# Attention and MLP on one core: who copies the sink probabilities, and how many steps the attention runs ahead

## The chip, the core and the metric

The program runs on one core of a Trainium2 chip. Times are device microseconds (us) of one execution; a kernel's time is the median of its runs. The engines are called as in the profile: PE (TensorE matmul), PEld (its weight load), DVE (VectorE), ACT (ScalarE), POOL (GpSimd) and SP (SyncE, which issues most DMAs).

## What is computed

A masked attention with 4 batches, 8 heads, 768 positions and head size 64, whose output is laid out as 3072 rows of 512 and put through an MLP:

```python
keep = is_sink | in_window            # 4 sink positions, window 128
scores = np.where(keep, q @ k.T / sqrt(64), -1e9)
a = softmax(scores)
x = (a @ v)  ->  (3072, 512)
h = x @ w_in                          # 512 x 2048
out = np.maximum(0.01 * h, h) @ w_out # 2048 x 512
```

## The kernel before

The rows are cut into eight **units** `u` of 384 rows (half of a batch, three tiles of 128 queries). A unit needs its attention for 8 heads, in 4 pairs, and then its MLP. The kernel writes both as Python generators, and every `yield` ends a **step**. PE executes its instructions in the order in which they are written (`tc.manual_schedule(engines=MANUAL)`); the order on DVE, ACT, POOL and SP is made at build time by a scheduler, which places instructions by its own forecast. At run time each engine takes its instructions strictly in that order.

*The MLP of a unit* (`mlp_stream`) goes through 16 blocks `fc` of 128 hidden columns. One block is seven steps: four of three matmuls into the PSUM tile `h` (L601), then three of three matmuls into `o` (L627) that use the block before. Between them ACT makes `g = 0.01 h` (L608), DVE `g = max(h, g)` (L609), ACT the rounded `gh` (L610), and DVE (POOL in unit 0) the rest `gl` (L611). `h` has one PSUM bank: the first matmul of the next `h` waits for L609 of this one. The names below give unit and block: `g3_2` is unit 3, block 2.

*The attention* (`attention_stream`) has 15 steps for a pair of heads: six `scores` (L293, then on DVE L311 and L319, on ACT `exp` L322, on DVE L323, L324, L328), six `tail` (a transpose L367 into `t`, L374 on ACT, L375 on DVE, L337 on POOL), one `sinks` (L388, L395, L408 to L410) and two `values` (L448 and L458 into `v`, then L462 on ACT and L463 on DVE to `xf`, and for the second head L465 on POOL, L467 on DVE, `xh` L557 on ACT and `xl` L558 on DVE). Units 0 and 1 have another, cheaper form of attention (L285, L305, L307, L490, L356, L359, L421, L425). Q, K and V of the later units are split into two parts by ACT and POOL (L243, L244, L246; L257, L258; L260, L261), with one buffer for `vsp` (L257) and `ssp` (L260).

*How the two are woven together* is a formula: after MLP step `x` the attention stream is advanced until it has made `due` steps.

```python
if x < mlp_steps:
    due = early_steps + LEAD0 + (early_steps + LEAD - LEAD0) * (x + 1) // mlp_steps
else:
    due = 2 * early_steps + LEAD + att_steps * (x + 1 - mlp_steps) // mlp_steps
```

Here `early_steps` is 32, `att_steps` 60, `mlp_steps` 112 and `LEAD0` 7. So 37 attention steps go into the MLP of unit 0, and 60 into each MLP of units 1 to 6, one after every 28/15 MLP steps. As 28 steps are four blocks and 15 steps are one pair, the picture repeats every four blocks: a pair's `values` stand at the same place of blocks 1 and 2, 5 and 6, 9 and 10, 13 and 14.

The copy that is changed stands in `tail`: after the last tile of a head it gathers the probabilities of the four sink columns from `pk` into `sk`, 128 x 8 or 128 x 12 elements, 48 times. `sk` is read by the transpose L388. In units 2 to 5, `check_weights` reads every weight again and tests its range (L194 on ACT, L196 on POOL, L198 on DVE, through two shared buffers), one weight block after each odd `fc`.

Of the kernel before, what the change touches and what calls it, by code (L numbers as in the profile page):

```python
# [27 lines left out]
T = 3  # L28
# [3 lines left out]
NSK = 4  # L32
# [8 lines left out]
MASKED = 1.0e38  # L41
DEEP = 9.0e8
SO = 3
LEAD = 12
LEAD0 = 7
SAHEAD = 2
NACT = 4
# [71 lines left out]
def fast_path(ctx, tc, cpool, qp, qk, vu, vs, w_in, w_out, out, ident, lims, negm, wmin, wmax):  # L119
    nc = tc.nc  # L120
# [214 lines left out]
    def place(out, src, x, prev):  # L335
        sign = -1 if prev else 1
        nc.gpsimd.affine_select(out=out, in_=src, pattern=([[0, x]] if x > 1 else []) + [[sign, P]],  # L337
                                base=-1 if prev else 0, channel_multiplier=-sign, compare_op=ALU.is_ge, fill=0.0)
# [4 lines left out]
    def slot():  # L343
        slots[0] += 1
        n = slots[0]
        if phase[0] == 0 and n % 2:
            return ps_h.tile([P, 512], F32, tag="h", name=f"t{n}")
        return ps_t.tile([P, 512], F32, tag="d" if phase[0] == 2 and n % 2 else "t", name=f"t{n}")
# [15 lines left out]
    def tail(u, h, j, pk, pt, sk):  # L364
        half = u % 2
        tp = slot()
        nc.tensor.transpose(out=tp[:, 0:P], in_=pk[:, j, NSK:], identity=ident)  # L367
        if j or half:
            o = 2 * P * j if half else (2 * j - 1) * P
            stg = apool.tile([P, 2, P], F32R, tag="stg", name=f"stg{u}_{h}_{j}")  # L370
            hi, lo = stg[:, 0, :], stg[:, 1, :]
        else:
            o, hi, lo = None, pt[:, 0, 0:P], pt[:, 1, 0:P]
        nc.scalar.copy(out=hi, in_=tp[:, 0:P])  # L374
        nc.vector.tensor_tensor(out=lo, in0=tp[:, 0:P], in1=hi.bitcast(F32), op=ALU.subtract)  # L375
        if o is not None:
            for prev in (1, 0):
                place(pt[:, :, o + (1 - prev) * P:o + (2 - prev) * P], stg, 2, prev)
        if j == T - 1:
            nj = T - 1 + half  # L380
            nc.vector.tensor_copy(out=sk[:, 0:nj, h % 2], in_=pk[:, T - nj:, 0:NSK])

    def sinks(u, pair, sk, state):
        half = u % 2
# [139 lines left out]
    def attend_late(u, h, pend, state):  # L524
        odd = h % 2
        sp = split_head(u, h)
        state = state[h // 2 % 2]
        if odd:
            state["v"] = split_values(u, h - 1)
        else:  # L530
            state["sk"] = apool.tile([P, T, 2, NSK], F32, tag="sk", name=f"sk{u}_{h // 2}")
        load_next(u, h)
        pk = apool.tile([P, T, WM], F32, tag="pk", name=f"pk{u}_{h}", bufs=PKB)
        sk = state["sk"]
        pt = apool.tile([P, 2, 2 * TU], F32R, tag="pt", name=f"pt{u}_{h}")
        state["pt", odd] = pt
        for j in range(T):
            ps = scores(u, h, j, (0, TU + NK[u % 2]), sp)
            softmax(u, h, j, ps, pk[:, j, :])
            yield  # L540
            at = len(pend) - (VSW and j == 0 and not odd and len(pend) > 0)
            pend.insert(at, (0, lambda j=j: tail(u, h, j, pk, pt, sk)))
# [123 lines left out]
    for x, _ in enumerate(mlp_stream()):  # L666
        if x >= mlp_steps:
            phase[0] = 2
# [4 lines that stand above are left out]
        while done < due:  # L673
# [204 lines left out]
```

## Time and profile before

| | |
|---|---|
| median of 3 runs | 699.86 us (699.4 to 700.22) |
| the profiled execution, its own time | 699.75 us |
| its span, first to last instruction | 698.0 us |
| PE busy / DVE / ACT / POOL | 98% / 77% / 62% / 57% of the span |
| granted clock of TensorE | 0.998 of full speed |
| MLP of unit 0 begins | 36.6 us |
| MLPs of units 1 to 7 begin (first L601 of each) | 125.8, 206.9, 291.3, 373.4, 458.1, 540.1, 621.8 us |

The share outside the span is 1.75 us. Matmuls are pipelined: a matmul of `h` is shown 0.34 us long, but the next one starts 0.175 us after it. So about 0.165 us of a wait of PE hide under the modelled end of the matmul before it.

### The profile page before, as it was taken

The numbers are of one execution on the slowest core, as the hardware profiler recorded it, in microseconds if no ns is written. First come the engines' busy times: TensorE is split into PE (matmuls) and PEld (weight loads), VectorE is DVE, ScalarE is ACT, GpSimd is POOL, SyncE is SP. The second block draws the span as 40 slices with busy tenths as digits, with TensorE's granted clock in tenths as the row PEclk, the third lists the DMA queues.
The fourth block names the chain that finished last, engine by engine and source line by source line (L and its number), as shares of the span: only waits on it lengthen the run. The fifth ranks groups of instructions, "written<-read, shape, count | busy, mean of one in ns | idle before, by whom it ended". The sixth has DMA issues, their size and how long they took to land.

```text
span 698.0 us, 12481 instructions
## 1 busy us (share of the span) xinstructions
PE 684.3 (98%) x3869; PEld 598.0 (86%) x3869; DVE 537.0 (77%) x1732; ACT 430.7 (62%) x1182; POOL 400.6 (57%) x550
## 2 busy tenths in 40 slices
PE   8999999999999999999999999999999999999996
PEld 5467788889998899988998899998999999899995
DVE  6999898666788898978898888887888988642322
ACT  6987676576666666667666667666676665522221
POOL 3357678465567877576775877757767665400000
PEclk9999999999999999999999999999999999999999
DMA  7865672212215423344333433333432310000001
GB/s 223 286 199 183 220 231 87 92 39 66 72 50 181 139 79 116 96 140 122 118 108 123 151 84 117 111 111 123 125 103 77 119 53 17 1 31 16 0 1 49
DMA packets 42599, 74.28 MB, mean 106 GB/s; under 512 B 3488, under 2 KB 26272, under 8 KB 42528
## 3 DMA queue, kind: packets, MB, share of 16 engines
q1 hardware_dynamic: 42384, 73.31, 33.3%
q8 instruction: 32, 0.52, 0.3%
q14 instruction: 39, 0.32, 0.2%
q10 hardware_dynamic: 144, 0.13, 0.1%
HBM read 67.14 MB, written 6.29 MB: 105 GB/s over the span
## 4 chain that ended last, share of the span: by engine, by line
PE 86%; DVE 5%; ACT 3%; POOL 2%; DMA 2%; issue 1%; POOLq 0%; ACTq 0%; SPq 0%; DVEq 0%
PE h L601 36%; PE o L627 34%; PE v L458 4%; PE s L293 4%; PE t L367 2%; PE v L421 1%; PE s L285 1%; ACT pe L307 1%; PE o_s L627 1%; PE o_o L627 1%; DMA ciraw<-in_w_in 1%; DVE pe L305 1%; ACT qksp L243 1%; DMA coraw<-in_w_out 1%; DVE g L609 0%
## 5 line engine op out<-in xcount | busy, mean ns | idle before, releaser
L601 PE MATMUL h<-xh,wi 128*128 128x384 f32 x1024 | 311.1, 352 | 1.9 <-DVE sm L323 1.2
L627 PE MATMUL o<-wo,gh 128*128 128x512 f32 x736 | 234.8, 400 | 0.2 <-ACT gh L610 0.2
L601 PEld LDWEIGHTS h<-xh,wi 128*128 128x128 f32 x1024 | 189.9, 188 | 17.4 <-issue 3.1
L601 PE MATMUL h<-xl,wi 128*128 128x384 f32 x512 | 172.8, 338 | 0.2 <-DVE xl L558 0.2
L337 POOL TENSOR_SCALAR_AFFINE_SELECT pt<-stg 128x256 fp32r<-128x256 f32 x240 | 101.1, 446 | 83.9 <-DVE stg L375 57.8
L627 PE MATMUL o<-wo,gl 128*128 128x512 f32 x368 | 145.4, 395 | 0.4 <-POOL gl L611 0.4
L627 PEld LDWEIGHTS o<-wo,gh 128*128 128x128 f32 x736 | 126.4, 188 | 16.7 <-issue 1.3
L609 DVE TENSOR_TENSOR g<-h,g 128x384 f32<-128x384 f32 x128 | 71.0, 555 | 54.9 <-ACT g L608 53.1
L608 ACT ACTIVATE g<-h 128x384 f32<-128x384 f32 x128 | 62.3, 487 | 66.5 <-PE h L601 65.8
L601 PEld LDWEIGHTS h<-xl,wi 128*128 128x128 f32 x512 | 96.9, 189 | 3.0 <-DVE xl L558 0.6
L610 ACT CAST gh<-g 128x384 fp32r<-128x384 f32 x128 | 65.2, 510 | 32.1 <-DVE g L609 30.6
L627 PEld LDWEIGHTS o<-wo,gl 128*128 128x128 f32 x368 | 69.1, 188 | 18.0 <-POOL gl L611 1.1
L322 ACT ACTIVATE pk<-pk,negm 128x128 f32<-128x128 f32 (+1 forms) x144 | 58.3, 405 | 36.8 <-DVE negm L319 35.9
L611 DVE TENSOR_TENSOR gl<-g,gh 128x384 fp32r<-128x384 f32 x112 | 69.8, 623 | 11.6 <-ACT gh L610 9.9
L244 POOL TENSOR_TENSOR qksp<-qkraw,qksp 64x392 fp32r<-64x392 f32 (+1 forms) x48 | 59.0, 1228 | 29.3 <-ACT qksp L243 16.2
L374 ACT CAST stg<-t 128x128 fp32r<-128x128 f32 x120 | 31.2, 260 | 53.0 <-PE t L367 50.5
L293 PEld LDWEIGHTS s<-qksp 128*128 128x128 f32 x288 | 53.3, 188 | 7.0 <-issue 0.6
L293 PE MATMUL s<-qksp 128*128 128x260 f32 (+1 forms) x288 | 56.2, 277 | 0.3 <-DVE negm L319 0.3
L328 DVE TENSOR_SCALAR pk<-pk,sm 128x132 f32<-128x132 f32 (+1 forms) x120 | 52.2, 435 | 3.1
L246 POOL TENSOR_TENSOR qksp<-qkraw,qksp 128x384 fp32r<-128x384 f32 x48 | 51.3, 1068 | 3.8
L311 DVE COPY_PREDICATED s<-tri,s 128x128 f32<-128x128 int8 x120 | 34.7, 289 | 16.6 <-PE s L293 15.4
L319 DVE CUSTOM_DVE_ANT_0 pk<-s,m 128x128 f32<-128x128 f32 (+1 forms) x144 | 41.7, 290 | 4.6 <-PE s L293 2.2
(149 smaller groups left out, 1119.7 us busy)
## 6 DMA issues: line engine op xcount, KB each, us to landing
qkraw<-in_qk SPq DMA_DIRECT2D x24, 454.0 KB, 3.3
qkraw<-in_qk SPq DMA_DIRECT2D x24, 388.0 KB, 3.1
wiraw<-in_w_in SPq DMA_DIRECT2D x16, 512.0 KB, 4.1
woraw<-in_w_out SPq DMA_DIRECT2D x16, 512.0 KB, 3.7
ciraw<-in_w_in SPq DMA_DIRECT2D x16, 512.0 KB, 3.7
coraw<-in_w_out SPq DMA_DIRECT2D x16, 512.0 KB, 3.5
out<-ob SPq DMA_DIRECT2D x23, 256.0 KB, 2.0
vraw<-in_vu SPq DMA_DIRECT2D x14, 256.0 KB, 2.6
```

The lines of the kernel that those rows point to most:

```text
L244: nc.gpsimd.tensor_tensor(out=sp[D:P, TU:TU + n], in0=raw[D:P, TU:TU + n], in1=sp[D:P, TU:TU + n].bitcast(F32), op=ALU.subtract)
L246: nc.gpsimd.tensor_tensor(out=sp[:, TU + n:2 * TU + n], in0=raw[:, 0:TU], in1=sp[:, 0:TU].bitcast(F32), op=ALU.subtract)
L293: nc.tensor.matmul(ps[:, 0:kn], lhsT=sp[:, off + j * P:off + (j + 1) * P], rhs=sp[:, TU + k0:TU + k0 + kn], start=c == 0, stop=c == len(pa ...
L322: nc.scalar.activation(out=w, in_=w, func=AF.Exp, scale=-1.0, bias=neg, accum_out=sm)
L328: nc.vector.tensor_scalar(out=w, in0=w, scalar1=sm, scalar2=None, op0=ALU.mult)
L337: nc.gpsimd.affine_select(out=out, in_=src, pattern=([[0, x]] if x > 1 else []) + [[sign, P]], base=-1 if prev else 0, channel_multiplier= ...
L601: nc.tensor.matmul(ph[:, 0:TU], lhsT=w[:, cs], rhs=x, start=cc == 0 and c == 0, stop=cc == NCC - 1 and c == 2)
L608: nc.scalar.mul(g, ph[:, 0:TU], 0.01)
L609: anchor[0] = nc.vector.tensor_tensor(out=g, in0=ph[:, 0:TU], in1=g, op=ALU.max)
L610: nc.scalar.copy(out=gh, in_=g)
L611: (nc.gpsimd if u == 0 else nc.vector).tensor_tensor(out=gl, in0=g, in1=gh.bitcast(F32), op=ALU.subtract)
L627: nc.tensor.matmul(acc, lhsT=gg[:, tsl], rhs=w[:, cs], start=f == 0 and c == 0, stop=f == NFC - 1 and c == 2)
```

## The change

Two lines. `LEAD` goes from 12 to 13: from unit 1 on the attention has made one step more at each MLP step, and unit 0 takes 38 attention steps, not 37. And the copy into `sk` is issued on ScalarE (ACT), not on VectorE (DVE). It stands in `tail`, which only units 2 to 7 use.

```diff
-LEAD = 12
+LEAD = 13
@@ tail
         if j == T - 1:
             nj = T - 1 + half
-            nc.vector.tensor_copy(out=sk[:, 0:nj, h % 2], in_=pk[:, T - nj:, 0:NSK])
+            nc.scalar.copy(out=sk[:, 0:nj, h % 2], in_=pk[:, T - nj:, 0:NSK])
```

What this does to the orders is seen best at the second `values` of a pair. On PE, in the MLP of unit 3 (block 2, with the attention of unit 4), before the change; `v4_1` is the second head's values, `s4_3_1` a score of the next pair, `h3_2` the block's hidden tile:

```order
L293 MATMUL s4_3_0_4201<-qksp4_3_4183 128x128 x2
L601 MATMUL h3_2_4169<-xh3_3_3935,wi2_633 128x384
L601 MATMUL h3_2_4169<-xl3_3_3936,wi2_633 128x384
L601 MATMUL h3_2_4169<-xh3_3_3935,wi2_633 128x384
L448 MATMUL t109_4220<-st0_100,ssp4_0_3889 128x256
L458 MATMUL v4_1_4222<-pt4_1_3901,vsp4_0_3888 128x256 x5
L627 MATMUL o3_0_4141<-wo1_548,gh3_1_4125 128x512 x2
```

The same place on PE with the change:

```order
L448 MATMUL t109_4210<-st0_100,ssp4_0_3883 128x256
L458 MATMUL v4_1_4212<-pt4_1_3895,vsp4_0_3882 128x256 x5
L601 MATMUL h3_2_4173<-xh3_3_3925,wi2_633 128x384
L601 MATMUL h3_2_4173<-xl3_3_3926,wi2_633 128x384
L601 MATMUL h3_2_4173<-xh3_3_3925,wi2_633 128x384
L293 MATMUL s4_3_1_4236<-qksp4_3_4177 128x260 x2
L627 MATMUL o3_0_4150<-wo1_548,gh3_1_4135 128x512 x2
```

The values have moved from behind the last matmuls of `h3_2` to before them, and the next score, formerly between the `o` matmuls, now follows `h3_2` directly.

On DVE, the instructions ahead of `g3_2` (L609, which frees the bank of `h3_2`), before the change:

```order
L198 ISA zeroi4_4165,wmin_64<-magi4_4164,zeroi4_4165 128x512
L198 ISA wmin_64 128x1
L375 TENSOR_TENSOR pt4_2_4020<-t108_4173,pt4_2_4020 128x128
L319 ISA pk4_3_4199,negm_63<-s4_3_0_4201,m0_115 128x128
L319 ISA negm_63 128x1
L609 TENSOR_TENSOR g3_2_4213<-h3_2_4169,g3_2_4213 128x384
```

With the change:

```order
L328 TENSOR_SCALAR pk4_3_4193<-pk4_3_4193,sm4_3_0_4198 128x128
L311 COPY_PREDICATED s4_3_1_4236<-tri_116,s4_3_1_4236 128x128
L319 ISA pk4_3_4193,negm_63<-s4_3_1_4236,m1_620 128x132
L319 ISA negm_63 128x1
L463 TENSOR_TENSOR xf4_0_4147<-v4_1_4212,xf4_0_4147 64x512
L609 TENSOR_TENSOR g3_2_4229<-h3_2_4173,g3_2_4229 128x384
```

The mask and maximum of the new score (L311, L319) and the sum of the values (L463) now stand ahead of L609; before, they stood behind it.

On ACT at the opening of unit 0's MLP (`gh0_0` is what the first `o` waits for), before the change:

```order
L608 ACTIVATE g0_0_659<-h0_0_646 128x384
L182 CAST wi2_633<-wif2_629 128x512
L359 COPY pt1_0_482<-t23_666 128x2x256
L490 ACTIVATE pe1_1_0_587<-pe1_1_0_587,sm1_1_585 128x260 x2
L610 CAST gh0_0_660<-g0_0_659 128x384
L490 ACTIVATE pe1_1_1_607<-pe1_1_1_607,sm1_1_585 128x260 x2
L608 ACTIVATE g0_1_709<-h0_1_693 128x384
```

With the change:

```order
L359 COPY pt1_0_482<-t23_656 128x2x256
L608 ACTIVATE g0_0_666<-h0_0_646 128x384
L182 CAST wi2_633<-wif2_629 128x512
L490 ACTIVATE pe1_1_0_587<-pe1_1_0_587,sm1_1_585 128x260 x2
L490 ACTIVATE pe1_1_1_607<-pe1_1_1_607,sm1_1_585 128x260 x2
L608 ACTIVATE g0_1_709<-h0_1_693 128x384
L610 CAST gh0_0_667<-g0_0_666 128x384
```

`gh0_0` has moved behind two more of the attention's scalings (L490) and behind L608 of the next block.

## Rows read from the trace of the kernel before

**Rows 1.** The page's line of busy times (us, share of the span, instructions), and busy time of each engine while the MLP of unit 0 runs (us and number of instructions for PE, PEld, DVE, ACT, POOL; then the granted clock, DMA share, GB/s).
```profile
PE 684.3 (98%) x3869; PEld 598.0 (86%) x3869; DVE 537.0 (77%) x1732; ACT 430.7 (62%) x1182; POOL 400.6 (57%) x550
...
36.50:125.70 89.20, 88.35 (x496) 70.78 (x497) 80.34 (x196) 64.90 (x161) 63.92 (x70) 1.00 0.57 180
```

**Rows 2.** What PE waited for between 200 and 620 us: who waits, for whom; us in total, times, the longest.
```profile
PE h L601 <- DVE sm L323: 1.2, 3, 0.5
PE t L367 <- DVE xf L467: 0.5, 1, 0.5
PE s L293 <- DVE negm L319: 0.3, 1, 0.3
PE h L601 <- DVE g L609: 0.2, 1, 0.2
PE v L458 <- DVE xf L463: 0.2, 1, 0.2
```

**Rows 3.** The timeline of one block of unit 7, where no attention is left: the last matmul of an `h`, what ACT and DVE do with it, and the first matmul of the next `h` (start us, duration us, engine, line, operation; in brackets the idle time before it and what ended it).
```profile
627.93 0.34 PE L601 MATMUL h<-xh,wi 128*128 128x384 f32 x1
...
628.37 0.49 ACT L608 ACTIVATE g<-h 128x384 f32<-128x384 f32 x1 [2.59 <-PE h L601]
...
628.89 0.56 DVE L609 TENSOR_TENSOR g<-h,g 128x384 f32<-128x384 f32 x1 [0.20 <-ACT g L608]
...
630.22 0.34 PE L601 MATMUL h<-xh,wi 128*128 128x384 f32 x1
```

**Rows 4.** The timeline around the wait at 312 us (unit 3, from block 3 to block 4): PE's score and the next `h`, and ACT just before.
```profile
311.46 0.33 PE L293 MATMUL s<-qksp 128*128 128x128 f32 x2
312.17 0.44 PE L601 MATMUL h<-xh,wi 128*128 128x384 f32 x1 [0.37 <-DVE sm L323]
...
309.88 0.51 ACT L557 CAST xh<-xf 128x384 fp32r<-128x384 f32 x1 [1.61 <-DVE xf L467]
310.30 0.84 ACT L243 CAST qksp<-qkraw 128x776 fp32r<-128x776 f32 x1
311.04 0.48 ACT L608 ACTIVATE g<-h 128x384 f32<-128x384 f32 x1
```

**Rows 5.** The timeline of the values' chain (PE, ACT and DVE, 303 to 308 us), and of PE over one block's `o` matmuls with one score and one transpose among them (from the last matmul of an `h`, at 563.07, to the first of the next).
```profile
303.84 0.75 PE L458 MATMUL v<-pt,vsp 128*128 128x256 f32 x5
...
305.19 0.51 ACT L257 CAST vsp<-vraw 128x384 fp32r<-128x384 f32 x1
305.73 0.58 ACT L462 COPY xf<-v 64x512 f32<-64x512 f32 x1
306.33 0.51 ACT L610 CAST gh<-g 128x384 fp32r<-128x384 f32 x1
...
306.27 0.30 DVE L311 COPY_PREDICATED s<-tri,s 128x128 f32<-128x128 int8 x1
306.60 0.69 DVE L463 TENSOR_TENSOR xf<-v,xf 64x512 f32<-64x512 f32 x1
307.32 0.30 DVE L319 CUSTOM_DVE_ANT_0 pk<-s,m 128x132 f32<-128x132 f32 x1
307.54 0.56 DVE L611 TENSOR_TENSOR gl<-g,gh 128x384 fp32r<-128x384 f32 x1
...
563.07 0.33 PE L601 MATMUL h<-xh,wi 128*128 128x384 f32 x1
...
565.61 0.42 PE L601 MATMUL h<-xh,wi 128*128 128x384 f32 x1
```

**Rows 6.** The timeline of the opening of unit 0's MLP: ACT, then POOL's first `gl`, then PE's first `o` matmul that reads it.
```profile
39.20 0.20 ACT L307 ACTIVATION_READ_ACCUMULATOR pe<-pe,negm 128x1 f32 x1
39.49 0.49 ACT L608 ACTIVATE g<-h 128x384 f32<-128x384 f32 x1
39.88 0.61 ACT L182 CAST wi<-wif 128x512 fp32r<-128x512 f32 x1
40.39 0.59 ACT L359 COPY pt<-t 128x512 f32<-128x512 f32 x1
40.87 0.92 ACT L490 ACTIVATE pe<-pe,sm 128x260 f32<-128x260 f32 x2
41.69 0.50 ACT L610 CAST gh<-g 128x384 fp32r<-128x384 f32 x1
...
42.27 1.01 POOL L611 TENSOR_TENSOR gl<-g,gh 128x384 fp32r<-128x384 f32 x1 [0.23 <-ACT gh L610]
...
43.33 0.51 PE L627 MATMUL o<-wo,gl 128*128 128x512 f32 x1 [0.36 <-POOL gl L611]
```

**Rows 7.** The copy into `sk`: all 48 (duration ns, least/median/most; first and last start, forms), and one that is long, on the timeline, with what POOL does beside it.
```profile
L381 DVE COPY sk<-pk x48: 157/368/1007, 110.3 to 603.5; 128x8 f32<-128x8 f32 x24, 128x12 f32<-128x12 f32 x24
...
571.88 1.00 DVE L381 COPY sk<-pk 128x12 f32<-128x12 f32 x1
...
571.49 1.36 POOL L246 TENSOR_TENSOR qksp<-qkraw,qksp 128x384 fp32r<-128x384 f32 x1
```

**Rows 8.** Two groups of ACT's instructions by line (number; busy us, mean ns of one; idle before them).
```profile
L322 ACT ACTIVATION_READ_ACCUMULATOR pk<-pk,negm 128x1 f32 x144 | 27.2, 189 | 0.0
L260 ACT CAST ssp<-vsraw 128x128 fp32r<-128x128 f32 x24 | 7.0, 290 | 2.0 <-DMA vsraw<-in_vs 2.0
```

**Rows 9.** One DVE and one ACT instruction of the weight check, on the timeline.
```profile
221.62 0.87 DVE L198 CUSTOM_DVE_ANT_0 zeroi<-magi,zeroi 128x512 f32<-128x512 f32 x1 [0.65 <-POOL zeroi L196]
...
224.19 0.67 ACT L194 ACTIVATE mago<-coraw 128x512 f32<-128x512 f32 x1 [1.76 <-DMA coraw<-in_w_out]
```

## The prediction

> **What bounds the kernel now.** I read the busy line first. PE works for 684.3 of 698.0 us; the next engine, DVE, reaches 77% [rows 1]. The change neither adds nor removes a PE instruction, so the time moves only by PE's waits. Next I read the waits by stage. Before the MLP of unit 0 PE waits for other engines, but there the change moves nothing: the attention of units 0 and 1 uses no copy into `sk`, and `LEAD` acts only inside the MLPs. From 200 to 620 us the list of PE's waits is short: three waits of a next `h` behind L323 (1.2 us together), one transpose behind L467 (0.5), one score behind L319 (0.3), one `h` behind L609 and one `v` behind L463 (0.2 each) [rows 2]. About 165 ns of each wait are hidden under the shown end of the matmul before it, so a wait that goes returns its shown length plus that.
>
> The resource behind most of these waits is the one bank of `h`, which I call the gate. Unit 7 without attention shows what it needs: last `h` matmul at 627.93, L608 at 628.37, L609 at 628.89 for 0.56 us. So the next `h` could start about 1.57 us after the last one; PE has other work until 630.22, 2.29 us after it [rows 3]. Some 0.7 us are to spare. Attention matmuls in the `o` steps make this more, and what ACT or DVE has queued ahead of L608 or L609 makes it less.
>
> **What it removes.** At 312 us the row names L323 as releaser, but that is only what came last on DVE. The timeline shows the cause: ACT stands in L557 at 309.88 after 1.61 us of waiting for L467, then does L243, and only at 311.04 starts L608, whose `g` the next `h` needs; PE stands 0.37 us [rows 4]. The same pattern, a pair's second `values` late against block 3, makes the other two of the three. With the change the values come ahead of the `h` matmuls of block 2 instead of behind them, some 0.7 us earlier against the gate of block 3 (four matmul slots), and L243 goes ahead of L557. I take all three as gone: 1.2 + 3 × 0.165 = 1.7 us. The transpose behind L467 (0.5 + 0.165), the score behind L319 (0.3 + 0.165) and the `v` behind L463 (0.2 + 0.165: two heads' values that stand 1.4 us apart after the change, with `o` matmuls between) depend on the same place: 0.64 + 0.47 + 0.34 with the list's roundings undone. The `h` behind L609 has L194 ahead of L608 in both orders and stays. Together **−3.15 us**.
>
> **What it adds.** (1) *The opening of unit 0.* PE now waits for `gl` until 43.33 [rows 6]. In the new order `gh0_0` stands behind L359, L182, two pairs of L490 and L608 of block 1. From the starts on the rows: L359 from 39.30 for 0.48, L608 for 0.39, L182 for 0.51, two pairs of L490 for 0.82 each, L608 for 0.39, which makes 42.71; L610 0.50 and 0.08 to POOL, `gl` 1.01, 0.05 to PE: 44.35. So **+1.0 us**, unless PE has other work there: the lower bound is 0, since the extra attention step fills a part that I can't place. DVE is busy for 80.34 of the 89.2 us of this stage and PE for 88.35 [rows 1], so what is lost at the start is hardly won back.
>
> (2) *The gate of blocks 2, 6, 10, 14.* Here the values stand directly ahead of the `h` matmuls, and the next pair's score directly behind them. Let S be the start of that score. One block with a score and a transpose takes 2.54 us from the last `h` to the next [rows 5], so without a wait the next `h` comes 2.54 − 0.175 = 2.365 after S. ACT: the values end at S − 0.38, L257 starts at S − 0.34 and takes 0.54 (305.19 to 305.73), L462 0.60 (to 306.33), so L608 can start at S + 0.80. DVE: L463 at S + 0.81, behind L462, takes 0.72 (306.60 to 307.32), L319 0.22 (307.32 to 307.54), so L609 starts at S + 1.75 [rows 5], ends 0.56 later [rows 3], and 0.06 later `h` can go: S + 2.37. In every second unit L319 stands ahead of L463, and it is S + 2.33. So 24 gates (four in each of six units) have nothing to spare, where before L463 stood behind L609. I take 0.03 us for each, **+0.7 us**. The ends are 0 (the hidden 165 ns cover it, as for every wait) and 0.15 each (one instruction more in the queue, half of an L311 of 0.30 us), 3.6 us.
>
> (3) *Two weight checks in such gates.* In unit 2 the check's L198 (0.87 us, [rows 9]) stands between L463 and L609 of block 2; its issue takes 0.76 of that, at a gate with nothing to spare: +0.7. In unit 4 an L194 (0.67, [rows 9]) stands between L462 and L608: L608 starts at about S + 1.45, which puts `h` some 0.3 late: +0.3. Together **+1.0 us**; lower bound 0, where such a check finds its data early and slips.
>
> (4) *The copy itself.* DVE loses 48 instructions of 157 to 1007 ns, at the median 368, 17.7 us together [rows 7]. ACT gains 48. No ACT copy of 128 x 8 is in this trace; the nearest rows are the read of an accumulator column, 189 ns, and a cast of 128 x 128, 290 ns [rows 8]: 9 to 14 us, I take 11. ACT works for 62% of the span. Most of the copies stand between L608 and L610 or between L462 and L610, where only `gh` comes later, and that is wanted a block later; `sk` is wanted by the `sinks` step, later still. So both sides are hidden: 0. Without the cover (a copy ahead of L608 at a tight gate) each would cost 0.2 to 0.3 us; in the order none stands there at blocks 2, 6, 10 or 14.
>
> The long copies on DVE stand beside POOL: 1.00 us at 571.88, inside L246 of 1.36 us from 571.49, against 157 ns at the least [rows 7]. The Trainium skill says why they might (SBUF — State Buffer, "Who interferes with whom": the port pair that DVE shares with GpSimd is an exclusive lock, and ACT has ports of its own); by that the move frees DVE of up to 0.85 us at each meeting, and the trace agrees in the two rows shown. Another page speaks against the move: Perfetto Trace Analysis, "Optimizing Scalar/DVE Operations", has the operation quicker on DVE where it has a fast mode, and offloading sensible where DVE is saturated. At 77% it isn't, so by this rule nothing is won, which is also what the gates above give.
>
> **Sum.** −3.15 + 1.0 + 0.7 + 1.0 + 0 = −0.45 us. The sum is made against the profiled execution's 699.75 us (span 698.0 and 1.75 around it), 0.11 below the median: **699.3 us**.
>
> **Rivals.** *Faster.* The opening's loss is taken up by other matmuls, and the 24 gates hide under the 165 ns: 699.3 − 1.0 − 0.7 = 697.6 us. For it: PE has 98% of work that can fill in, and the gates come out at the edge, not beyond. Against it: in the opening PE already waits 0.36 us for this `gl` [rows 6], so no other matmul is ready in its order; DVE's queue in the MLPs holds more than I counted. It wins from 0.85 us saved on these terms. Chance 0.30.
>
> *Slower.* The 24 gates are late by 0.15 us or more, since L463 and L319 now stand ahead of L609 and any instruction of DVE that lasts longer than its row (as the copy's 157 to 1007 ns, [rows 7]) shows in full: 3.6 in place of 0.7, which is 702.2 us. Within the measurement's bound it decides from about 0.11 us a gate (24 × 0.11 = 2.6, which puts the sum at 701.3). For it: L467, L328 and L311 share the same stretch of DVE. Against it: the removed copies make room on DVE. Chance 0.13.
>
> *The waits only change place.* The late values hit another gate instead of block 3 of units 3 to 5, and the 1.7 us come back: 699.3 + 1.7 = 701.0. Or nothing moves on PE's path at all, 699.75. Both end in "same", with the sum itself: 0.57 together.
>
> **How the numbers follow.** About 0.2% (1.4 us) is what a measurement of this kernel can tell from no change: faster is under 698.46, slower over 701.26. The likeliest is the sum, −0.06% to the profiled execution. The faster rival reaches to 697.6, and with the checks' 1.0 us hidden too to 696.6; the slower one from 701.3 to 702.2. Leaving out about 1 in 10 at either end, the range is 697.2 to 701.3 us. Faster 0.30, within the bound 0.57, slower 0.13.
>
> **What would show it.** Right: the list of PE's waits from 200 to 620 us has no `t` behind L467 and no `h` at block 3 of units 3 to 5; PE's first `o` matmul that reads `gl` starts near 44.35, not 43.33; `h` waits by some hundredths behind blocks 2, 6, 10 and 14 and by 0.3 to 0.7 us in unit 2 and unit 4 there; L381 on ACT lasts 0.19 to 0.29 us. Wrong on the fast side: the MLP of unit 0 begins and ends when it did, and no `h` waits follow a score after values. Wrong on the slow side: a row of `h` behind L609 with some 24 waits of over 0.1 us. The forecast fails also if the scheduler's order makes DVE wait for a copy on ACT before the `sinks` transposes, which shows as a wait of L388 for L381.

## The result, and the profile after

The changed kernel takes 705.92 us (median of 6 runs, 704.57 to 708.15), the kernel before 699.80 beside it: ratio 1.0092, 95% interval 1.0082 to 1.0101. That is 6.1 us slower; the forecast was 699.3 (697.2 to 701.3), no change. The profiled execution shown here is the slowest of the six (708.15 us, span 706.4; the others' spans are 702.8 to 705.4), and the text says where that matters. Its granted clock is also the lowest, 0.994 on average; the fastest of the six (704.57 us) has 1.000, so 4.8 us are lost with the clock up, too.

The first matmul of `h` of each unit marks where the time came in (length of each unit's MLP in us, from its first `h` matmul to that of the next unit; worked out from the traces):

| | start | u0 | u1 | u2 | u3 | u4 | u5 | u6 | u7 and tail |
|---|---|---|---|---|---|---|---|---|---|
| before | 36.57 | 89.19 | 81.11 | 84.49 | 82.00 | 84.74 | 82.02 | 81.69 | 76.2 |
| after | 36.63 | 92.52 | 81.31 | 87.36 | 82.17 | 84.73 | 83.76 | 82.04 | 75.9 |

So 3.3 us were lost in unit 0, 2.9 in unit 2, 1.7 in unit 5, and 0.2 to 0.35 in units 1, 3 and 6.

The page's busy line after, which answers to [rows 1]:

```profile
PE 687.2 (97%) x3869; PEld 597.2 (85%) x3869; DVE 517.8 (73%) x1684; ACT 445.6 (63%) x1230; POOL 400.7 (57%) x550
```

And PE's waits from 200 to 620 us (who, for whom: us in total, times, the longest), which answer to [rows 2]:

```profile
PE h L601 <- DVE sm L323: 4.3, 5, 2.1
PE v L458 <- DVE xf L463: 0.5, 2, 0.3
```

The transpose behind L467 and the score behind L319 are gone, as forecast, and so are the three waits at block 3. The `h` behind L609, which the forecast kept, is gone too. The `v` behind L463, which it took as gone, is not: it stood at 609.33 us (0.18) and stands at 617.02 (0.28), around block 13 of unit 6; a second one came at 476.98. In the place of the others `h` waits five times, and for 4.3 us. DVE has lost 19 us of work and ACT has gained 15; what that is worth on PE is measured below (the copy alone).

The opening of unit 0 (timeline: ACT, POOL, PE), to be held against [rows 6]:

```profile
39.36 0.58 ACT L359 COPY pt<-t 128x512 f32<-128x512 f32 x1
39.82 0.50 ACT L608 ACTIVATE g<-h 128x384 f32<-128x384 f32 x1
40.21 0.63 ACT L182 CAST wi<-wif 128x512 fp32r<-128x512 f32 x1
40.71 1.74 ACT L490 ACTIVATE pe<-pe,sm 128x260 f32<-128x260 f32 x4
42.34 0.49 ACT L608 ACTIVATE g<-h 128x384 f32<-128x384 f32 x1
42.71 0.52 ACT L610 CAST gh<-g 128x384 fp32r<-128x384 f32 x1
...
43.31 1.01 POOL L611 TENSOR_TENSOR gl<-g,gh 128x384 fp32r<-128x384 f32 x1 [0.60 <-ACT gh L610]
...
43.28 0.73 PE L627 MATMUL o<-wo,gh 128*128 128x512 f32 x2 [1.57 <-ACT gh L610]
44.38 0.50 PE L627 MATMUL o<-wo,gl 128*128 128x512 f32 x1 [0.36 <-POOL gl L611]
```

L610 starts at 42.71 and the first `gl` matmul at 44.38; the forecast worked out 42.71 and 44.35. But PE has now stood for 1.57 and 0.36 us within 3 us, and in this execution its clock fell behind that (windows of this kernel: us, busy time and number of PE, PEld, DVE, ACT, POOL, then granted clock, DMA share and GB/s):

```profile
43.20:46.00 2.80, 2.36 (x9) 1.25 (x10) 2.66 (x5) 1.62 (x4) 2.69 (x3) 0.95 0.57 187
46.00:49.20 3.20, 3.20 (x11) 2.27 (x11) 3.10 (x10) 2.17 (x7) 2.39 (x3) 0.51 0.96 306
49.20:55.00 5.80, 5.80 (x41) 4.55 (x42) 3.73 (x7) 3.15 (x8) 2.24 (x4) 1.00 0.66 217
228.80:232.50 3.70, 3.70 (x16) 3.61 (x17) 3.10 (x11) 3.10 (x8) 3.51 (x6) 0.67 0.54 182
```

0.51 is the lower of the two levels, 1.2 GHz, for 3.2 us: 11 matmuls where the same stretch at full clock has 26 (below). It happened again behind the wait at 228 us. Unit 2 lasts 87.36 us here, and 86.08 to 86.24 in three of the runs below that make the same thirteenth step and whose clock stayed up there, so this second fall costs about 1.2 us.

The third loss of unit 0 (after the opening and the clock) is at block 11 (timeline: ACT's `gh`, POOL, PE):

```profile
107.54 0.51 ACT L610 CAST gh<-g 128x384 fp32r<-128x384 f32 x1
...
108.13 1.03 POOL L244 TENSOR_TENSOR qksp<-qkraw,qksp 64x392 fp32r<-64x392 f32 x1
109.24 1.01 POOL L246 TENSOR_TENSOR qksp<-qkraw,qksp 128x384 fp32r<-128x384 f32 x1
110.21 1.00 POOL L611 TENSOR_TENSOR gl<-g,gh 128x384 fp32r<-128x384 f32 x1
...
111.27 0.50 PE L627 MATMUL o<-wo,gl 128*128 128x512 f32 x1 [1.13 <-POOL gl L611]
```

`gh` is ready at 108.05, but POOL does L244 and L246 of the next head first, which stood behind this `gl` before. PE stands 1.13 us, which with the hidden part is 1.3.

The longest wait of the later units, block 2 of unit 2 (ACT, DVE, PE):

```profile
224.56 0.67 ACT L194 ACTIVATE magi<-ciraw 128x512 f32<-128x512 f32 x1 [1.33 <-DMA ciraw<-in_w_in]
...
225.41 0.62 ACT L257 CAST vsp<-vraw 128x512 fp32r<-128x512 f32 x1
226.05 0.58 ACT L462 COPY xf<-v 64x512 f32<-64x512 f32 x1
226.65 0.49 ACT L608 ACTIVATE g<-h 128x384 f32<-128x384 f32 x1
...
227.38 0.69 DVE L198 CUSTOM_DVE_ANT_0 zeroi<-magi,zeroi 128x512 f32<-128x512 f32 x1
...
228.12 0.56 DVE L609 TENSOR_TENSOR g<-h,g 128x384 f32<-128x384 f32 x1
...
228.73 0.45 PE L601 MATMUL h<-xh,wi 128*128 128x384 f32 x1 [2.12 <-DVE sm L323]
```

L323 is again only what came last on DVE. What is late is L609, which ends at 228.68: behind L198, behind L463 (226.66), behind L462, behind L194, which waited 1.33 us for its load. In unit 5 (ACT, PE) an L194 stands ahead of L257 and L462 in the same way:

```profile
479.07 0.67 ACT L194 ACTIVATE mago<-coraw 128x512 f32<-128x512 f32 x1 [0.56 <-DVE sm L324]
...
482.20 0.45 PE L601 MATMUL h<-xh,wi 128*128 128x384 f32 x1 [1.40 <-DVE sm L323]
```

How much of such a wait is the load varies. With LEAD 13 alone (a run below), L194 waits 0.29 us at the gate in unit 2 (ACT, DVE, PE):

```profile
222.23 0.68 ACT L194 ACTIVATE magi<-ciraw 128x512 f32<-128x512 f32 x1 [0.29 <-DMA ciraw<-in_w_in]
...
225.07 0.69 DVE L198 CUSTOM_DVE_ANT_0 zeroi<-magi,zeroi 128x512 f32<-128x512 f32 x1
...
226.41 0.44 PE L601 MATMUL h<-xh,wi 128*128 128x384 f32 x1 [1.17 <-DVE sm L323]
```

Here the two instructions themselves, 0.68 and 0.69 us, come to about what the gate is late, 1.17 and the hidden 0.165.

The copy itself (instruction group; duration least, median, most):

```profile
L381 ACT COPY sk<-pk x48: 181/198/202, 110.7 to 610.7; 128x8 f32<-128x8 f32 x24, 128x12 f32<-128x12 f32 x24
```

198 ns, at the low end of the forecast's 189 to 290 [rows 8], and never long, where DVE's copies took up to 1007 ns [rows 7].

### The profile page after: what moved, and what is told of

It reads as the page before. It is cut to its first block, busy times and chain, and to the rows that moved or that the text cites. A ratio compares the mean times of both kernels' runs of the same rounds, so it can differ in the third digit from the quotient of the medians.

```text
span 706.4 us, 12437 instructions
## 1 busy us (share of the span) xinstructions
PE 687.2 (97%) x3869; PEld 597.2 (85%) x3869; DVE 517.8 (73%) x1684; ACT 445.6 (63%) x1230; POOL 400.7 (57%) x550
## 5 line engine op out<-in xcount | busy, mean ns | idle before, releaser
L601 PE MATMUL h<-xh,wi 128*128 128x384 f32 x1024 | 318.9, 351 | 5.1 <-DVE sm L323 4.3
L627 PE MATMUL o<-wo,gh 128*128 128x512 f32 x736 | 240.4, 408 | 1.6 <-ACT gh L610 1.6
L337 POOL TENSOR_SCALAR_AFFINE_SELECT pt<-stg 128x256 fp32r<-128x256 f32 x240 | 109.2, 480 | 55.4 <-DVE stg L375 32.2
L609 DVE TENSOR_TENSOR g<-h,g 128x384 f32<-128x384 f32 x128 | 70.9, 554 | 62.7 <-ACT g L608 62.2
L608 ACT ACTIVATE g<-h 128x384 f32<-128x384 f32 x128 | 62.3, 486 | 78.0 <-PE h L601 77.3
L610 ACT CAST gh<-g 128x384 fp32r<-128x384 f32 x128 | 65.6, 513 | 28.0 <-DVE g L609 26.9
L611 DVE TENSOR_TENSOR gl<-g,gh 128x384 fp32r<-128x384 f32 x112 | 71.9, 642 | 11.8 <-ACT gh L610 11.1
L244 POOL TENSOR_TENSOR qksp<-qkraw,qksp 64x392 fp32r<-64x392 f32 (+1 forms) x48 | 56.9, 1186 | 30.9 <-issue 17.3
L311 DVE COPY_PREDICATED s<-tri,s 128x128 f32<-128x128 int8 x120 | 34.7, 289 | 25.4 <-PE s L293 23.8
L328 DVE TENSOR_SCALAR pk<-pk,sm 128x132 f32<-128x132 f32 (+1 forms) x120 | 50.9, 424 | 2.9
L243 ACT CAST qksp<-qkraw 128x776 fp32r<-128x776 f32 (+1 forms) x48 | 42.9, 894 | 14.4 <-PE s L293 12.1
L246 POOL TENSOR_TENSOR qksp<-qkraw,qksp 128x384 fp32r<-128x384 f32 x48 | 49.4, 1029 | 3.8
L323 DVE TENSOR_SCALAR sm<-sm 128x1 f32<-128x1 f32 x144 | 21.4, 148 | 38.6 <-ACT pk L322 37.8
```

The lines of the kernel that those rows point to most:

```text
L244: nc.gpsimd.tensor_tensor(out=sp[D:P, TU:TU + n], in0=raw[D:P, TU:TU + n], in1=sp[D:P, TU:TU + n].bitcast(F32), op=ALU.subtract)
L246: nc.gpsimd.tensor_tensor(out=sp[:, TU + n:2 * TU + n], in0=raw[:, 0:TU], in1=sp[:, 0:TU].bitcast(F32), op=ALU.subtract)
L328: nc.vector.tensor_scalar(out=w, in0=w, scalar1=sm, scalar2=None, op0=ALU.mult)
L601: nc.tensor.matmul(ph[:, 0:TU], lhsT=w[:, cs], rhs=x, start=cc == 0 and c == 0, stop=cc == NCC - 1 and c == 2)
L608: nc.scalar.mul(g, ph[:, 0:TU], 0.01)
L609: anchor[0] = nc.vector.tensor_tensor(out=g, in0=ph[:, 0:TU], in1=g, op=ALU.max)
```

## The experiments

**Which of the two edits.** LEAD 13 alone, and the copy alone:

```diff
-LEAD = 12
+LEAD = 13
```

> The kernel before with LEAD 13 and nothing else; the copy into sk stays on DVE. Theory 1 (the extra step is the cause: in unit 0 it moves gh0_0 and one gl back, in units 1 to 6 it puts the values ahead of the h matmuls of blocks 2, 6, 10 and 14): as slow as the changed kernel, ratio 1.006 to 1.010, 704 to 707 us, with the long waits of h at block 2 of units 2 and 5. Theory 2 (the copy on ACT is the cause: it stands in the queue ahead of L608): like the kernel before, 699 to 700 us.

```diff
-            nc.vector.tensor_copy(out=sk[:, 0:nj, h % 2], in_=pk[:, T - nj:, 0:NSK])
+            nc.scalar.copy(out=sk[:, 0:nj, h % 2], in_=pk[:, T - nj:, 0:NSK])
```

> The kernel before with the copy on ACT and LEAD 12. Theory 1 (the extra step is the cause): 699.0 to 700.0 us, ratio 0.999 to 1.000, since L381 on ACT (0.20 us) is hidden. Theory 2 (the copy is the cause): 704 to 707 us, and L381 is found directly ahead of the L608 that a wait of h ends on.

LEAD 13 alone: 705.36 us, ratio 1.0095 (1.0081 to 1.0109). The copy alone: 699.04 us, 0.9993 (0.9984 to 1.0002). The extra step is the cause; the copy changes nothing that is clear of the interval. Both came out in the range of the first theory.

The profiled execution of LEAD 13 alone (PE's timeline) has the waits of the opening to 10 ns, and the clock did not fall:

```profile
43.29 0.73 PE L627 MATMUL o<-wo,gh 128*128 128x512 f32 x2 [1.57 <-ACT gh L610]
44.38 0.50 PE L627 MATMUL o<-wo,gl 128*128 128x512 f32 x1 [0.36 <-POOL gl L611]
```

Its window behind them (columns as above):

```profile
46.00:49.20 3.20, 3.20 (x26) 2.32 (x26) 3.10 (x10) 2.16 (x7) 2.40 (x3) 1.00 0.97 298
```

Its unit 0 lasts 91.11 us against 92.52 with the fall. That prices it: 1.4 us, in some executions and not in others (the run without the range test, below, has the same two waits and the fall). Unit 0 without the fall loses 91.11 − 89.19 = 1.9 us.

**Unit 0.** The thirteenth step is made only when unit 1 begins:

```diff
-            due = early_steps + LEAD0 + (early_steps + LEAD - LEAD0) * (x + 1) // mlp_steps
+            due = early_steps + LEAD0 + (early_steps + 12 - LEAD0) * (x + 1) // mlp_steps
```

> The changed kernel, but unit 0 takes 37 attention steps as before and the thirteenth step is made at the start of unit 1. Theory 1 has two parts. In unit 0 the profile of the changed kernel lost 3.3 us (opening 1.0, the gl at 111 us 1.3, a stretch at the lower clock): they come back, so the MLP of unit 1 begins near 125.8 us, the granted clock stays 1.00 in 43 to 50 us, and the time is 702 to 703 us. Rival: the opening's delay is worked off elsewhere, and the time stays at 705 to 706 us.

703.37 us (702.99 to 703.85), 2.55 less than the changed kernel; unit 0 lasts 88.87 us (89.19 before), unit 1 begins at 125.48. That is about 0.4 us over the expected range, but the delay of unit 0 is not worked off elsewhere.

The same with the extra step made in block 5:

```diff
-            due = early_steps + LEAD0 + (early_steps + LEAD - LEAD0) * (x + 1) // mlp_steps
+            due = early_steps + LEAD0 + (early_steps + 12 - LEAD0) * (x + 1) // mlp_steps + (x >= 40)
```

> The changed kernel, 38 attention steps in unit 0 as there, but the extra one is made at MLP step 40 (block 5) and not at the start. The orders have gh0_0 where it was before, and L244 and L246 ahead of the gl of block 11 on POOL as in the changed kernel. The two waits of unit 0 are told apart: the first gl matmul at 43.4 us as before, no stretch at the lower clock behind it, and a wait of 1.0 to 1.2 us for gl at 109 to 111 us; MLP of unit 1 from 126.8 to 127.1 us, time 704.3 to 705 us. If the opening's delay were worked off by the end of unit 0, unit 1 would begin as in the run with LEAD 13 alone, at 127.7 us.

704.12 us. The first `gl` matmul came at 43.41 and the clock stayed up, as expected. The wait for `gl` at block 11 didn't come, which the expectation missed: against the changed kernel one of the two L183 ahead of L244 has moved behind that `gl`. A shorter one (0.45 us) came at 124.45 instead, and unit 1 began at 126.21, 0.6 us earlier than expected. So the run doesn't take the opening away alone. Block 10 tells the two apart, as it lies behind the opening and ahead of the wait at block 11. Its first `gl` matmul in the kernel before, with LEAD 13 alone and in this run (PE's timeline):

```profile
102.83 0.39 PE L627 MATMUL o<-wo,gl 128*128 128x512 f32 x1
...
103.93 0.39 PE L627 MATMUL o<-wo,gl 128*128 128x512 f32 x1
...
102.97 0.39 PE L627 MATMUL o<-wo,gl 128*128 128x512 f32 x1
```

The opening's 1.05 us are still there at block 10 with LEAD 13 alone, and not in this run: they are a loss by themselves.

**The range test of the weights.** The changed kernel and the kernel before without it:

```diff
-            if 2 <= u < 6 and fc % 2:
+            if False:
```

> The changed kernel without the range test of the weights in units 2 to 5 (L194, L196, L198 and their loads are left out, and its two result columns are filled with 1.0). Theory 1a (the long waits of h at block 2 of units 2, 4 and 5 come from L194, which stands ahead of L257, L462 and L608 and waits for its data): the waits of 2.1, 1.4 and 0.4 us go, and with them the stretch at the lower clock behind the first: 700 to 701.5 us. Theory 1b (the gates are late through the values alone, L463 ahead of L609): the time stays above 703 us and waits of over 1 us remain at block 2.

> The kernel before without the range test of the weights (L194, L196, L198 and their loads left out, the two result columns filled with 1.0): the control for the run that left the test out of the changed kernel and gained 6.2 us. Theory 1a (the test costs only where the extra step has put it ahead of a tight gate): little is gained, 698.5 to 699.7 us. Rival (the test costs about the same in both kernels and says nothing of the change): 693 to 695 us.

The changed kernel without the test: 699.69 us (698.37 to 702.26), a little under the expected range. All waits of `h` after 130 us are gone; what is left from there to 618 us is

```profile
PE v L458 <- DVE xf L463: 0.3, 1, 0.3
```

I first read this as proof that the test hurts only where the extra step puts it. The control refuted that: the kernel before without the test takes 694.85 us (0.9931, 0.9918 to 0.9945), 5.0 us less, and its list from 130 to 618 us is

```profile
PE v L458 <- DVE xf L463: 0.2, 1, 0.2
```

So the other six waits of [rows 2], five of which the forecast put down to late values, come with the test as well. Both kernels pay for it, one 5.0 and the other 6.2 us.

Both causes taken away (37 steps in unit 0, no test), and the same with LEAD 12 and the copy on ACT:

> The changed kernel with 37 attention steps in unit 0 and without the range test of the weights (left out as before). If the opening of unit 0 and the test ahead of the gates are the whole loss, both gains add: 698.4 us of the run without the test and without the lower clock, less the 2.3 to 3.3 us of unit 0, 695 to 696.5 us, and no wait of PE over 0.15 us from 130 us on. If a third cause is there, 698 us or more.

> LEAD 12 with the copy on ACT, without the range test of the weights (left out, its result columns filled with 1.0). With 694.85 us for the same with the copy on DVE, and 696.73 us with LEAD 13 from unit 1 on, it tells whose the 1.9 us between them are. If the values ahead of h at blocks 2, 6, 10 and 14 cost them (0.1 us at each gate): 694.3 to 695.3 us. If the copy on ACT costs them: 696.3 to 697 us.

696.73 us and 694.06 us, the one 0.2 us over its range, the other 0.2 under. So LEAD 13 costs in the later units even where nothing waits visibly. Unit by unit (u1 to u6) the difference is 0.19, 0.42, 0.12, 0.45, 0.04 and 0.39, together 1.6 us. The medians are 2.7 us apart; in the two traces the rest, 1.1 us, lies behind the last matmul (6.39 us against 5.33), a stretch that lasts 5.3 to 7.0 us from one trace to the next, so 1.6 is what is shown of the gates. The gate of block 2 of unit 2 in the first of the two shows how (DVE, PEld, PE):

```profile
222.38 0.56 DVE L609 TENSOR_TENSOR g<-h,g 128x384 f32<-128x384 f32 x1
...
222.99 0.19 PEld L601 LDWEIGHTS h<-xh,wi 128*128 128x128 f32 x1 [0.27 <-DVE sm L323]
222.99 0.44 PE L601 MATMUL h<-xh,wi 128*128 128x384 f32 x1
223.10 0.19 PEld L601 LDWEIGHTS h<-xl,wi 128*128 128x128 f32 x1
223.27 0.34 PE L601 MATMUL h<-xl,wi 128*128 128x384 f32 x1
223.44 0.34 PE L601 MATMUL h<-xh,wi 128*128 128x384 f32 x1
```

L609 ends at 222.94, `h` starts 0.05 later: the gate opens just when PE arrives, as the forecast worked out. PE isn't listed as waiting, but its second matmul follows after 0.28 us instead of 0.175. The rows of PEld show where that goes: the first matmul's weight load starts only at the release, together with the matmul, and the second's 0.17 us ahead of its matmul. In this trace that 0.1 us is found at blocks 2, 6 and 10 of the even units and at block 14 of the odd ones, where L609 ends 0.06 to 0.08 us before PE starts. At the other gates of the odd units it ends 0.12 to 0.13 before, and 0.03 to 0.04 us are lost. The copy on ACT is not to blame: with LEAD 12 it is there too.

**The place of the test.** Two edits at once: L194 is queued behind L608 of its own block, and the first load comes at the end of unit 0 (37 steps in unit 0, LEAD 13 from unit 1):

```diff
+                gate[0] = nc.scalar.mul(g, ph[:, 0:TU], 0.01)
@@ check_weights
-            pace(dma, anchor[0])
+            pace(dma, decoded[-1])
-        nc.scalar.activation(out=mag, in_=raw.bitcast(F32)[:, :, 1], func=AF.Abs,
+        with tc.issue_after(gate[0].ins): nc.scalar.activation(out=mag, in_=raw.bitcast(F32)[:, :, 1], func=AF.Abs,
```

> The changed kernel with 37 attention steps in unit 0, nothing left out, but L194 of each test is queued on ACT behind L608 of its own block, so that it can't stand directly ahead of L257, L462 and the next L608, and the first of its loads is issued at the end of unit 0. Theory 1a (what cost was L194 at that place, waiting for its load): close to the kernel without the test, 695.5 to 698 us, which is faster than both kernels. Rival (the test's work on ACT, DVE and POOL delays the gates wherever it stands): 701 us or more.

698.33 us (698.03 to 699.07, 11 runs), ratio 0.9978 (0.9969 to 0.9987), a little above the expected range: 5.0 us less than with the test in its old place, and faster than both kernels. Which of the two edits gives how much of it was not measured. PE's list from 130 to 618 us:

```profile
PE h L601 <- DVE sm L323: 0.8, 2, 0.5
PE h L601 <- DVE g L609: 0.3, 1, 0.3
PE v L458 <- DVE xf L463: 0.3, 1, 0.3
```

With the copy on DVE it is the same within the interval (698.56 us):

> LEAD 13 from unit 1 on, L194 behind L608 and the first load early, as in the run of 698.3 us, but with the copy on DVE. Tells what the copy on ACT is worth with the thirteenth step. If it is hidden on either engine: 697.8 to 698.8 us. If it is the copy on ACT that made that kernel fast: 700 us or more.

The same two edits with LEAD 12, the copy on ACT and then on DVE:

> The kernel with the copy on ACT and LEAD 12, with the same two edits to the test (L194 behind L608 of its block, first load early). It tells whether the thirteenth step is worth anything at all when its side effects are gone. If the extra step removes the waits at block 3 as forecast (3 us), this one stays 1 to 3 us slower than the same with the thirteenth step: 698 to 699.5 us. If the waits at block 3 came from the test too, it is as fast: 695.5 to 698 us.

> The kernel before (copy on DVE, LEAD 12) with L194 behind L608 of its block and the first load early. The run of the same with the copy on ACT took 706.5 us: there 15 L608 stand directly behind L381, which waits 0.8 us a time for L328, and PE waits 15 times for L463. If the copy on ACT in that place is the cause, this one has none of these waits and comes to 695.5 to 698 us, faster than both kernels. If the test's new order is the cause, it stays at 703 us or more.

706.51 and 707.71 us. The first is outside both of its ranges. I then blamed L381, which stands directly ahead of 15 L608 there; the second has no L381 on ACT and is as slow, which refutes that and is what its rival (the test's new order) expected. Its rows (POOL, DVE and PE in unit 3, block 10) show what happens:

```profile
345.86 0.69 DVE L198 CUSTOM_DVE_ANT_0 zeroi<-magi,zeroi 128x512 f32<-128x512 f32 x1
345.91 1.81 POOL L244 TENSOR_TENSOR qksp<-qkraw,qksp 64x524 fp32r<-64x524 f32 x1
346.48 1.33 DVE L328 TENSOR_SCALAR pk<-pk,sm 128x132 f32<-128x132 f32 x1
347.73 0.55 DVE L611 TENSOR_TENSOR gl<-g,gh 128x384 fp32r<-128x384 f32 x1
348.20 0.67 DVE L463 TENSOR_TENSOR xf<-v,xf 64x512 f32<-64x512 f32 x1
348.93 0.86 PE L458 MATMUL v<-pt,vsp 128*128 128x256 f32 x5 [0.71 <-DVE xf L463]
```

L198 has pushed L328 to where POOL runs L244; L328 takes 1.33 us and ends 0.09 after L244 ends, L463 is late behind it, and the `v` of the pair's second head waits, 14 times (8.9 us in all). Before 12 of the 14 stands such an L328, 1.05 to 1.34 us long.

Then the test after even blocks instead of odd ones, with LEAD 12 and with 13:

```diff
-            if 2 <= u < 6 and fc % 2:
+            if 2 <= u < 6 and fc % 2 == 0:
```

> LEAD 12, copy on ACT, the range test of the weights one block earlier (after each even block, not after each odd one). If the place of the test within the four blocks of a pair decides its cost, this differs from the 699.0 us of the same kernel with the test after odd blocks by over 2 us, to either side (694.1 us without the test is the floor); most of its L194 stand two instructions ahead of L608 of blocks 1 and 3, none directly ahead, so I expect 695 to 698 us. If the test costs its 5 us anywhere: 698.5 to 700 us.

> The changed kernel with 37 attention steps in unit 0 and the test after even blocks (703.4 us with the test after odd ones, 696.7 us without it). L194 of blocks 2 and 6 is four to six instructions ahead of the next L608, but the two tests at the start of a unit still stand between L608 of blocks 1 and 2. If the waits at block 2 come from these first two alone: 702 to 704 us with waits over 0.3 us at block 2 of units 2 to 5 only. If the place of every test counts: under 701 us or over 705 us.

703.72 and 717.94 us. Earlier by one block the test costs more with either LEAD. The gain expected of the first was a miss; the second came out as expected if the place of every test counts. And the test spread over units 2 to 7 (the flag that reads its results is worked out after block 13 of unit 7, not block 8):

```diff
+            n = 4 * (u - 2) + fc // 4 if 2 <= u < 7 and fc % 4 == 0 else 20 + fc if u == 7 and fc < 12 else -1
+            if n >= 0:
+                check_weights("io"[n % 2], n // 2)
@@ mlp_stream, the flag
-            if u == NU - 1 and fc == NFC // 2:
+            if u == NU - 1 and fc == 13:
```

> LEAD 12, copy on ACT, 20 tests one after each fourth block (0, 4, 8, 12) of units 2 to 6, the other 12 in unit 7, where PE has no attention and 0.7 us to spare at each block; the flag is worked out after block 13 of unit 7. If a test costs about 0.15 us among the attention (5 us over 32) and nothing in unit 7: 697 us. If the place counts, it is nearer to the 694.1 us without the test, since most L194 then stand ahead of L608 of blocks 1, 5, 9 and 13, where the trace of before has 0.9 us of cover: 695 to 696.5 us.

> The same with the 20 tests after blocks 2, 6, 10 and 14: most L194 stand ahead of L608 of blocks 3, 7 and 11, where little is to spare. If the place counts: 698 us or more, and waits of h behind blocks 3, 7 and 11. If it does not: like the run with blocks 0, 4, 8 and 12, within 0.7 us.

706.78 and 704.72 us (the second run has the 20 tests after blocks 2, 6, 10 and 14). The first is far above its range; the second is in its open one (698 or more), but its waits are not behind the blocks that it named. Unit 7 with its 12 tests lost 6.2 and 7.3 us up to its last matmul, the 20 tests among the attention 5.7 and 3.4 (against the same kernel without the test). L194 waits 2.1 us for its load ahead of L608 in unit 7 (656.10 us in the first), although nothing else is in ACT's way, `h` waits 1.74 us behind it, and behind that the granted clock is 0.50 from 660.8 to 664.0 us. My view that unit 7 has room for tests was wrong: it has room on the engines, not in the order.

The 32 tests do the same work wherever they stand. Their cost in units 2 to 5, from the unit lengths (one trace each) against the same kernel without them:

| | after odd blocks | after even blocks | odd, L194 behind L608, first load earlier |
|---|---|---|---|
| LEAD 12 | 4.5 (DVE copy), 5.5 (ACT copy) | 7.8 | 12.9 (DVE copy), 12.5 (ACT copy) |
| LEAD 13 from unit 1 | 6.9 | 20.4 | 2.2 |

Place and LEAD together decide it, from 2 to 20 us, not the amount of work.

## Why the prediction was wrong

The step that failed most is (3), the checks ahead of the gates, put at +1.0 us: with what the change removes it was to give −2.15 us, and the two gave +2.4. Next comes (1), put at +1.0 us for the opening of unit 0 alone; the unit lost 1.9 us, and 3.3 with the fall of the clock.

*What it removes (−3.15 us).* Five of the six waits that were named went; the `v` behind L463 (0.34 of the sum) stayed. It stands at the last pair of the attention, around block 13 of unit 6, where the picture does not repeat. But the cause of the others was not the values' place alone: without the test they are not there. The rows showed L557, L243 and L608 in a queue [rows 4] and I stopped at them, though the tests are in the same queue. What was won at block 3 came back at block 2, where an L194 now stands ahead of L257 and L462.

*The opening of unit 0 (+1.0).* Right, place and size: 44.38 for 44.35, 1.05 us. Two things were missing. POOL's order at block 11 (L244 and L246 ahead of `gl`) makes PE wait 1.3 us; the working followed PE, DVE and ACT at the opening and took the rest of unit 0 as unchanged. And the clock's fall behind the opening costs 1.4 us in executions that have it. The range left both out.

*The gates of blocks 2, 6, 10 and 14 (+0.7).* The step was right: they come out within hundredths of zero. Measured without the test: 1.6 us, since a gate that opens just in time still costs 0.1 us in the even units, and 0.03 to 0.04 at most of the odd ones. Inside the stated bounds (0 to 3.6). There are 23 such gates, not 24: unit 6 takes the last 47 attention steps and not 60, so it has no values at block 14.

*The two checks (+1.0).* This is the step that failed most. I counted the duration of L198 in unit 2 and of L194 in unit 4 and gave 0 as the other end. Measured at these gates with the hidden part: 2.3 us in unit 2, 0.6 in unit 4 and, in unit 5, where I had counted none, 1.6; gates of 0.3 us more at block 2 of unit 3 and at later blocks. I left out two things. In units 2 and 5 an L194 stands ahead of L257, L462 and L608 of block 2; the sum starts L257 right behind the values. And L194 can wait for its load, so that everything behind it on ACT waits too. At a gate that has nothing to spare both reach PE. In the trace shown the wait was 1.33 us; with LEAD 13 alone it was 0.29, and the place of L194 and L198 was nearly all. In unit 5 the row does not name the load. A row for such a wait stood in the text already: L194 with 1.76 us of idle time for its load [rows 9]. I used its duration and not its bracket. The +2.4 us are what the test costs more with LEAD 13 than in the kernel before (6.9 against 4.5 by the unit lengths; 6.6 against 5.1 by the medians).

*The copy (0).* Right: 699.04 against 699.70 beside it, and with LEAD 13 705.92 against 705.36; both signs, neither clear.

*The slower rival* named the right gates and the wrong mechanism. It wanted 0.15 us at each of 24 gates; what decided was three gates of 0.6 to 2.3 us and unit 0.

By the profile units 0 to 6 lose 8.65 us: opening 1.05, POOL's order 1.3 and the clock 1.4 in unit 0 (less 0.4 that is won back by its end), 1.6 at the gates, 1.2 from the clock in unit 2, and the rest, 2.5, from the test's place. By the medians: 2.55 us in unit 0 (the run that gives them back), and 3.6 us in the units behind, of which 1.9 are there without the test too (696.73 against 694.85 us). Not settled is why the clock falls in one execution and not in the next with the same waits to 10 ns, and with which place the test would cost nothing.

## What to carry to other kernels

Where PE is busy for 98% and gates have no slack, moving one stream by one step against another can re-deal every queue, as it did here: all engines' orders have to be compared over the whole stage, POOL's too, not only at the place that the change is about. An instruction that waits for a load costs its wait besides its duration to everything behind it in its queue, so an item that is off the path (a test, a check) should be followed in the queue, and measured by taking it out of both kernels: out of the changed one alone it would have been blamed for the whole loss.

## What the runs showed of the hardware

- The same pair of PE waits (1.57 and 0.36 us within 3 us) was followed by 3.2 us at a granted clock of 0.51 in one trace (the changed kernel) and 0.52 in another (without the test), and by 1.00 in a third (LEAD 13 alone).
- Where the release of a first `h` comes 0.06 us before it starts, behind an `o` matmul, the second `h` follows after 0.28 instead of 0.175 us, though no wait is listed; the first one's weight load started only at the release (222.99 us).
- L328 (128 x 132, SBUF to SBUF on DVE) took 0.27 to 0.29 us where POOL was idle and 1.33 beside POOL's L244, ending 0.09 us after it. The Trainium skill, SBUF — State Buffer, "Who interferes with whom", says that `tensor_scalar` on DVE can take the port pair it shares with GpSimd, and that the second to come is blocked for the whole instruction; the rows agree.
